# Top-k attention and two gated layers: transposes of later batches' keys written into the next block's search

## The chip, the core and the metric

The kernel runs on one core of a Trainium2 chip. The metric is the time of one execution in device microseconds (us). The core has TensorE (PE: matmuls and transposes), VectorE (DVE), ScalarE (ACT) and GpSimd (POOL); SyncE (SP) issues every DMA of this kernel, in one queue, in order. Matmuls write PSUM; the other engines copy from there to SBUF.

## What is computed

```python
scores = (q @ k^T) / sqrt(64)                  # 4 batches, 8 heads, 576 rows, head size 64
kth    = 32nd largest score of each row
attn   = softmax(where(scores >= kth, scores, -1e9))
x      = (attn @ v), laid out as 2304 rows x 512
y      = (sigmoid(x @ w_gate) * (x @ w_val)) @ w_out     # 512 -> 1536 -> 512
out    = relu(y @ w_in)**2 @ w_out2                      # 512 -> 2048 -> 512
```

## The kernel before

The 2304 rows are 18 tiles of 128 rows, grouped in 12 chunks (chunks 0 to 5 of one tile, 6 to 11 of two). In each chunk, attention goes over four pairs of heads. A **unit** is one row tile and one head: its scores (tile `sp`, L376) are copied to SBUF by ScalarE (`S`, L379), and VectorE searches them in a **block** of four maxima of eight (L392) with three replacements between (L399). Then come exponentials (ScalarE) and, from chunk 6 on, a split into float16 parts that ends as a DMA with transposition (`PT<-S`, L459), whose result is multiplied with the values (`xp`, L509). The two layers of chunk ci (`pg`, `pv`, `acc` in L753 and L793; `x2pq`, `ph`, `acc` in L825, L858 and L879) run on TensorE between the units of later chunks; their scaling needs squares on ScalarE (L823) that `x2pq` sums.

Before a batch's keys can be used, they are **prepared** once for each pair of heads by `prep_keys`: SP loads them (`kn` and the ends `ke`, L151 and L153), TensorE transposes them (`kpt`, L164: four transposes of 128 keys and one of 64), ScalarE rounds them to a high part (`kp`, L171), VectorE takes the low part (written over `kn`, L172), and SP stores both to DRAM (`ks`, L178). Units then load them as `kst` (L328). Batches 2 and 3 are prepared while chunks 6 and 8 are in attention, at the head of each pair of heads: eight preparations. They are called the first to the fourth (batch 2, TensorE at 438 to 524 us) and the fifth to the eighth (batch 3).

What sets the order: the program is traced as written, and a scheduler then places each instruction by priorities and by a timeline of its own; every engine and the DMA queue run what they were given in that order. A tile's name (its tag) has a fixed number of buffers: `S` has five, shared by the scores of units, by `kn` and by the values being prepared (`vm`); `kst` has three, shared by loaded keys and by `kp`; `qn` has two, shared by queries and `ke`. With five `S` buffers, `kn` of a preparation takes the buffer that the unit four blocks back gives up, when its transposing DMA has landed.

From chunk 6 on, the work traced with block n is put into its search by `late(marks)`, called once the four maxima exist (`marks`): first the float16 split of unit n-1, then `head(n + 1)` with the loads and scores of the next unit and with any preparation, then the values' preparation (`vn`, behind the fourth maximum), then the products of unit n-2. `add_manual_dep(..., NOSYNC)` orders two instructions for the scheduler; no engine waits for it on the chip.

Of the kernel before, what the change touches and what calls it, by code (L numbers as in the profile page):

```python
# [18 lines left out]
NOSYNC = mybir.DependencyInfo(mybir.DependencyClass.NoSync, mybir.DependencyReason.DATA)  # L19
# [39 lines left out]
MUP = 200.0  # L59
WSLOTS = 35  # L60
PREF = 4
YMOD = 0
LOP = 3
LOA = 0
# [9 lines left out]
def tile_topk_attention__then__two_moe_layers(  # L74
# [14 lines left out]
    nc = tc.nc  # L89
# [52 lines left out]
    kscr = {}  # L142
    kloc = {}

    def prep_keys(b, hp, keep=False):

        src = k[b, 2 * hp : 2 * hp + 2]
        kn = apool.tile([P, S], F32, tag="S", bufs=SB, name=f"kn_{b}_{hp}")
        kv = kn[:, 0 : CB * P].rearrange("p (c h d) -> p c h d", c=CB, h=2)
        for j in range(2):  # L150
            nc.sync.dma_start(kv[:, :, j], src[j, 0:SM].rearrange("(p c) d -> p c d", c=CB))  # L151
        ke = apool.tile([ST, 2, D], F32, tag="qn", bufs=2, name=f"ke_{b}_{hp}")
        nc.sync.dma_start(ke, src[:, SM:S].rearrange("h p d -> p h d"))  # L153
        kh = apool.tile([P, S], F32R, tag="kst", bufs=KST, name=f"kp_{b}_{hp}")
        kl = kn.bitcast(F32R)
        if keep:
            kl = mpool.tile([P, S], F32R, tag="m4", bufs=M4, name=f"kl_{b}_{hp}")
            kloc[(b, hp)] = (kh, kl)
        for lo, hi in ((0, CB), (CB, NB)):
            pt = ps_t.tile([P, 512], F32, tag="tr", name=f"kpt_{b}_{hp}_{lo}")  # L160
            w = 0
            for c in range(lo, hi):
                kp = P if c < CB else ST
                nc.tensor.transpose(  # L164
                    pt[:, w : w + kp],
                    (kv[:, c] if c < CB else ke).rearrange("p h d -> p (h d)"),
                    ident[0:kp, 0:kp],
                )
                w += kp
            c0 = lo * P  # L170
            nc.scalar.copy(kh[:, c0 : c0 + w], pt[:, 0:w])  # L171
            nc.vector.tensor_tensor(  # L172
                kl[:, c0 : c0 + w], pt[:, 0:w], kh[:, c0 : c0 + w], op=ALU.subtract
            )
        d = dpool.tile([2, 2, D, S], F32R, name=f"ks_{b}_{hp}", tag=f"ks_{b}_{hp}")
        for a, t in enumerate((kh.bitcast(F32), kl.bitcast(F32))):
            for j in range(2):
                nc.sync.dma_start(d.bitcast(F32)[j, a], t[j * D : (j + 1) * D])  # L178
        for j in range(2):
            kscr[(b, 2 * hp + j)] = d[j].rearrange("a d s -> (a d) s")  # L180
# [830 lines left out]
    def attention():  # L1011
# [21 lines left out]
        def head(n):  # L1033
# [3 lines left out]
            if j == 0 and i == 0:  # L1037
# [12 lines left out]
                for b in due:  # L1050
                    if (b, pr.hp) not in vscr:
                        prep_values(b, pr.hp)
                    if (b, pr.hp) not in done:
                        done.add((b, pr.hp))
                        prep_keys(b, pr.hp)
                if pr.ci == KEYS1 and (1, pr.hp) not in done:
                    done.add((1, pr.hp))
                    prep_keys(1, pr.hp)
# [58 lines left out]
        for n, (pr, pi, j, i) in enumerate(units):  # L1117
# [6 lines left out]
            if pr.ci >= TCI - 2:  # L1124

                def late(marks, n=n, pr=pr):
                    if units[n - 1][0].ci >= TCI:
                        turn(n - 1, marks[2])
                    if pr.ci >= TCI:
                        head(n + 1)  # L1130
                        if units[n - 1][0].ci < TCI:
                            tail(n - 1)
                    while late_values:
                        split_values(*late_values.pop(0), marks[3])
                    if units[n - 2][0].ci >= TCI:
                        tail(n - 2, marks[3])
# [153 lines left out]
```

## Time and profile before

| | |
|---|---|
| three runs | 1262.53, 1262.6 and 1261.23 us; median 1262.53 us |
| profiled execution | its span, first to last instruction, is 1261.3 us; the profile gives no other time for it |
| busy share of the span | PE 93%, DVE 76%, POOL 67%, ACT 66% |
| chain that ended last | PE 67%, ACT 9%, POOL 7%, DVE 7%, DMA 5% of the span |

The span is what the profiler saw on the core; the runs are timed without it. A busy share is an average over stages: VectorE's last search starts at 1070.92 us, and what follows its end is the last chunk's two layers on TensorE.

### The profile page before, as it was taken

The page shows a single profiled execution, that of the slowest core. Times are in us where ns is not written, and L with a number is a line of the kernel's source. Part 1 is how long each engine was busy: PE and PEld are TensorE (multiplying, and loading weights), DVE is VectorE, ACT ScalarE, POOL GpSimd, SP SyncE. Part 2 cuts the span into 40 slices and gives each one's busy share as a digit, 9 for nine tenths or more (in the row PEclk, how much of TensorE's full clock was granted, in tenths as well). Part 3 has the DMA queues.
Part 4 walks back from the last instruction along what each step waited for, and adds up shares of the span by engine and source line. Part 5 has one row for each costly group of instructions (what it writes and reads, how often), then busy time and mean ns, then how long its engine had stood idle before and what let it go on. Part 6 is the DMA issues. An engine that isn't in the chain of part 4 may idle for free.

```text
span 1261.3 us, 30690 instructions
## 1 busy us (share of the span) xinstructions
PE 1176.1 (93%) x11477; PEld 957.5 (76%) x11477; DVE 954.8 (76%) x1965; ACT 828.6 (66%) x1719; POOL 846.5 (67%) x1294
## 2 busy tenths in 40 slices
PE   6757989999889998899998999999999999999998
PEld 5536877987777877779787778877876887787775
DVE  6998789899977978899988899999789969110010
ACT  4998996577767676677776777776567657322122
POOL 1788774488876577797876987797678659425223
PEclk9986999999989999999999999999999999999999
DMA  7988762223344356665776575567434523200000
GB/s 188 366 298 275 260 199 81 59 76 90 113 131 130 81 125 159 143 136 130 137 157 133 125 181 115 127 140 158 77 73 97 116 54 60 53 2 1 17 1 18
DMA packets 243190, 153.94 MB, mean 122 GB/s; under 512 B 193120, under 2 KB 209504, under 8 KB 243040
## 3 DMA queue, kind: packets, MB, share of 16 engines
q1 hardware_dynamic: 243040, 151.97, 47.7%
q8 instruction: 91, 1.49, 0.5%
q14 instruction: 59, 0.48, 0.1%
HBM read 105.51 MB, written 18.09 MB: 98 GB/s over the span
## 4 chain that ended last, share of the span: by engine, by line
PE 67%; ACT 9%; POOL 7%; DVE 7%; DMA 5%; issue 3%; SPq 2%; POOLq 0%; ACTq 0%; DVEq 0%
PE ph L858 12%; PE acc L879 12%; PE acc L793 8%; PE pg L753 8%; PE pv L753 8%; PE sp L376 5%; PE xp L509 3%; DMA PT<-S 3%; DVE mx L392 2%; PE xp L536 2%; DVE W L399 2%; PE pg L912 1%; PE qpt L336 1%; PE ph L959 1%; PE acc L976 1%
## 5 line engine op out<-in xcount | busy, mean ns | idle before, releaser
L392 DVE MAX8 mx<-W 128x8 f32<-128x576 f32 x432 | 327.9, 759 | 11.2
L399 DVE MATCH_REPLACE8 W<-mx,W 128x576 f32<-128x576 f32 x288 | 213.8, 742 | 0.0
L858 PE MATMUL ph<-x,wi_w 128*128 128x256 f16 (+1 forms) x1920 | 190.9, 253 | 2.7 <-ACT x L832 2.6
L879 PE MATMUL acc<-w_w,rh 128*128 128x512 f16 x768 | 182.2, 379 | 0.9 <-POOL rh L871 0.9
L858 PEld LDWEIGHTS <-wi_w 128*128 128x128 f16 x1920 | 156.4, 99 | 29.0 <-issue 4.0
L753 PE MATMUL pg<-xs,wg_w 128*128 128x256 f16 (+1 forms) x1440 | 148.4, 254 | 1.1 <-ACT th L763 0.8
L753 PE MATMUL pv<-xs,wv_w 128*128 128x256 f16 (+1 forms) x1440 | 143.8, 252 | 5.1 <-DVE th L765 3.7
L376 PE MATMUL sp<-kst,qt 128*128 128x288 f32 x608 | 132.9, 330 | 6.5 <-ACT rh L869 2.5
L457 POOL TENSOR_TENSOR S<-W,S 128x512 f16<-128x512 f32 x192 | 137.0, 735 | 2.1
L379 ACT COPY S<-sp 128x576 f32<-128x576 f32 x144 | 91.8, 638 | 66.3 <-PE sp L376 39.7
L793 PEld LDWEIGHTS <-wo_w 128*128 128x128 f16 x1440 | 119.6, 99 | 19.2 <-issue 7.4
L411 ACT ACTIVATE W<-S,mx 128x576 f32<-128x576 f32 x144 | 111.8, 776 | 30.9 <-DVE mx L392 30.5
L753 PEld LDWEIGHTS <-wg_w 128*128 128x128 f16 x1440 | 118.9, 99 | 17.2 <-issue 1.4
L753 PEld LDWEIGHTS <-wv_w 128*128 128x128 f16 x1440 | 117.4, 98 | 18.1 <-issue 5.8
L765 DVE TENSOR_TENSOR th<-pv,th 128x512 f32<-128x512 f32 (+1 forms) x60 | 34.7, 579 | 125.4 <-PE pv L753 121.0
L879 PEld LDWEIGHTS <-rh 128*128 128x128 f16 x768 | 72.0, 98 | 73.3 <-POOL rh L871 1.2
L392 DVE MAX8 mx<-S 128x8 f32<-128x576 f32 x144 | 107.3, 745 | 25.9 <-ACT S L379 24.1
L793 PE MATMUL acc<-gh,wo_w 128*128 128x256 f16 (+1 forms) x1104 | 105.6, 250 | 4.7 <-ACT gh L768 2.6
L399 DVE MATCH_REPLACE8 W<-mx,S 128x576 f32<-128x576 f32 x144 | 106.9, 742 | 0.0
L455 POOL TENSOR_SCALAR W<-W,bs 128x576 f32<-128x576 f32 x96 | 71.6, 746 | 52.6 <-ACT S L454 47.8
L870 POOL TENSOR_TENSOR r<-r 128x512 f32<-128x512 f32 (+1 forms) x80 | 69.6, 869 | 54.8 <-ACT rh L869 54.1
L376 PEld LDWEIGHTS sp<-kst,qt 128*128 128x128 f32 x608 | 90.8, 192 | 17.5 <-issue 3.8
(246 smaller groups left out, 2331.5 us busy)
## 6 DMA issues: line engine op xcount, KB each, us to landing
kst<-ks SPq DMA_DIRECT2D x112, 288.0 KB, 3.1
v<-vd SPq DMA_DIRECT2D x32, 320.0 KB, 3.3
qn<-in_q_dram SPq DMA_DIRECT2D x128, 64.0 KB, 2.3
wi_r<-in_moe_w_in_dram SPq DMA_DIRECT2D x16, 512.0 KB, 6.2
w_r<-in_moe_w_out_dram SPq DMA_DIRECT2D x16, 512.0 KB, 4.5
v<-in_v_dram SPq DMA_DIRECT2D x56, 128.0 KB, 2.4
wg_r<-in_moe_w_gate_dram SPq DMA_DIRECT2D x12, 512.0 KB, 6.0
wv_r<-in_moe_w_val_dram SPq DMA_DIRECT2D x12, 512.0 KB, 7.3
```

What stands on the lines that cost most here:

```text
L376: nc.tensor.matmul(sp[:, e, 0:HALF], l, r, start=(x == 0), stop=(x == len(ops) - 1))
L379: nc.scalar.copy(ss.rearrange("p (e s) -> p e s", e=2), sp[:, :, 0:HALF])
L392: m8 = nc.vector.max(mx[:, min(r, 1)], cur)
L399: nc.vector.match_replace(wk, mx[:, min(r, 1)], cur, NEG)
L411: nc.scalar.activation(wk, ss, AF.Prelu, bias=kth, scale=-1.0, alpha=1.0 / BIG)
L455: nc.gpsimd.tensor_scalar(wk, wk, rz, 1.0, op0=ALU.mult, op1=ALU.mult)
L457: nc.gpsimd.tensor_tensor(pp[:, o : o + e - f], wk[:, f:e], pp[:, f:e], op=ALU.subtract)
L753: nc.tensor.matmul(pp[:, e * N : (e + 1) * N], wblk(wd, a, c, f0, P), xs[:, b_, c, :], start=(e == 0 and n == 0), stop=(n == 3 * KM - 1), ...
L793: nc.tensor.matmul(accs[d // 2][:, (d % 2) * N : (d % 2 + 1) * N], wblk("wo", a, f, d * P, P), gh[:, b_, e * N : (e + 1) * N], start=(f == ...
L858: nc.tensor.matmul(ph[:, e * N : (e + 1) * N], wblk("wi", a, c, f0, P), x2[:, b_, c, :], start=(e == 0 and n == 0), stop=(n == 3 * KM - 1) ...
L870: nc.gpsimd.tensor_tensor(r, r, r, op=ALU.mult)
L879: nc.tensor.matmul(acc2[i][:, 0:DM], gh[:, b_, e * N + i * P : e * N + (i + 1) * P], wblk("w2", a, f, 0, DM), start=(f == 0 and x == 0), s ...
```

## The change

`prep_keys` is cut in two for the preparations of batches 2 and 3 (`late=LATEK`): the loads stay where they were, and `split_keys` (transposes, rounding, low part, stores) is called in the same block's `late`, behind `head(n + 1)`, with the first transpose ordered behind the third maximum of block n (`marks[KMARK]`). So `kp` takes its buffer of tag `kst` after the keys that `head(n + 1)` loads, not before.

```diff
+LATEK = 1
+KMARK = 2
...
-    def prep_keys(b, hp, keep=False):
+    def prep_keys(b, hp, keep=False, late=False):
...
         nc.sync.dma_start(ke, src[:, SM:S].rearrange("h p d -> p h d"))
+        if late:
+            late_keys.append((b, hp, kn, kv, ke))
+        else:
+            split_keys(b, hp, kn, kv, ke, keep=keep)
+
+    late_keys = []
+
+    def split_keys(b, hp, kn, kv, ke, keep=False, after=None):
+
         kh = apool.tile([P, S], F32R, tag="kst", bufs=KST, name=f"kp_{b}_{hp}")
...
-                nc.tensor.transpose(
+                mm = nc.tensor.transpose(
...
+                if after is not None:
+                    tc.add_manual_dep(mm.ins, after.name, NOSYNC, reason="landed by then")
+                    after = None
...
-                        prep_keys(b, pr.hp)
+                        prep_keys(b, pr.hp, late=LATEK)
...
+                    while late_keys:
+                        split_keys(*late_keys.pop(0), after=marks[KMARK])
                     while late_values:
```

Nothing is removed or added in count on the compute engines. The order is the same up to the first preparation. In names, the first number of `kn`, `ke`, `kpt`, `kp`, `ks`, `vm`, `ve` is the batch and the second the pair of heads; in `S`, `sp`, `PT` it is row tile and head; `kst` begins with the chunk; the last number only counts.

The DMA queue at the first preparation (loads of `kn_2_0`, batch 2, pair 0); before:

```order
L151 DMA kn_2_0_5957<-in_k_dram 128x4x64 x2
L153 DMA ke_2_0_5960<-in_k_dram 64x2x64
L196 DMA ve_2_0_5948<-in_v_dram 64x2x64 x2
L310 DMA v_6_0_1_5710<-vd_1_0_3603 128x1280
L300 DMA qn_6_1_5979<-in_q_dram 128x2x64 x2
L300 DMA qn_7_1_5982<-in_q_dram 128x2x64 x2
L178 DMA ks_2_0_5974<-kp_2_0_5962 64x576 x2
L178 DMA ks_2_0_5974<-kn_2_0_5957 64x576 x2
L328 DMA kst_6_1_1_5987<-ks_1_0_773 128x576
L328 DMA kst_6_2_1_6121<-ks_1_1_973 128x576
```

and after the change:

```order
L342 DMA kst_6_1_1_5970<-ks_1_0_773 128x576
L330 DMA v_5_3_1_5348<-in_v_dram 128x256
L333 DMA v_5_3_1_5348<-in_v_dram 64x64
L330 DMA v_5_3_1_5348<-in_v_dram 128x256
L333 DMA v_5_3_1_5348<-in_v_dram 64x64
L207 DMA vm_2_0_5945<-in_v_dram 128x256 x2
L153 DMA kn_2_0_5957<-in_k_dram 128x4x64 x2
L155 DMA ke_2_0_5960<-in_k_dram 64x2x64
L210 DMA ve_2_0_5948<-in_v_dram 64x2x64 x2
L324 DMA v_6_0_1_5710<-vd_1_0_3603 128x1280
L314 DMA qn_6_1_5962<-in_q_dram 128x2x64 x2
L342 DMA kst_6_2_1_6121<-ks_1_1_973 128x576
```

The load of the second head's keys (`kst_6_1`) stood behind the stores of the first preparation and now stands ahead of its loads.

TensorE at the same preparation, from the last of the sums `x2pq` on; before:

```order
L825 LDWEIGHTS ones_86
L825 MATMUL x2pq_3_5654<-x2_3_5653,ones_86 128x128
L477 MATMUL tp_5_6_5997<-ident_81,W_5_6_5846 128x128 x4
L214 LDWEIGHTS ones_86
L214 MATMUL vn_2_0_6012<-vs_2_0_5953,ones_86 128x1
L214 LDWEIGHTS ones_86
L214 MATMUL vn_2_0_6012<-vs_2_0_5953,ones_86 128x1
```

and the scores of head 1 of the same row tile, 50 rows further down:

```order
L858 LDWEIGHTS wi_w0_2973
L858 MATMUL ph_3_1_5745<-x2_3_5653,wi_w0_2973 128x128
L858 LDWEIGHTS wi_w0_2973
L858 MATMUL ph_3_1_5745<-x2_3_5653,wi_w0_2973 128x128
L376 MATMUL sp_6_1_6124<-kst_6_1_1_5987,qt_6_0_1_5819 128x288 x4
L536 MATMUL xp_5_3_6141<-PE_5_3_6137,v_5_3_1_5348 64x128 x2
```

after the change, from the same sum on:

```order
L839 LDWEIGHTS ones_86
L839 MATMUL x2pq_3_5654<-x2_3_5653,ones_86 128x128
L390 MATMUL sp_7_1_6339<-kst_6_1_1_5970,qt_7_0_1_5941 128x288 x4
L228 LDWEIGHTS ones_86
L228 MATMUL vn_2_0_6012<-vs_2_0_5953,ones_86 128x1
L228 LDWEIGHTS ones_86
L228 MATMUL vn_2_0_6012<-vs_2_0_5953,ones_86 128x1
L491 MATMUL tp_5_7_6131<-ident_81,W_5_7_5986 128x128 x4
```

Scores of a later unit (`sp_7_1`) now stand between the sums and `vn`, those of `sp_7_0` between the last transposes of the preparation, and `sp_6_1` stands some 190 rows earlier than it did.

The DMA queue at the second preparation (`kn_2_1`); before:

```order
L196 DMA ve_2_2_6861<-in_v_dram 64x2x64
L459 DMA_TRANSPOSE PT_6_0_6229<-S_6_0_5989 128x9x128
L196 DMA ve_2_2_6861<-in_v_dram 64x2x64
L151 DMA kn_2_1_6392<-in_k_dram 128x4x64 x2
L459 DMA_TRANSPOSE PT_6_1_6336<-S_6_1_6123 128x9x128
L328 DMA kst_6_3_1_6422<-ks_1_1_973 128x576
L300 DMA qn_7_2_6417<-in_q_dram 128x2x64 x2
L459 DMA_TRANSPOSE PT_7_0_6371<-S_7_0_6231 128x9x128
L178 DMA ks_2_1_6409<-kp_2_1_6397 64x576 x2
L178 DMA ks_2_1_6409<-kn_2_1_6392 64x576 x2
```

after:

```order
L155 DMA ke_2_1_6395<-in_k_dram 64x2x64
L314 DMA qn_6_2_6397<-in_q_dram 128x2x64 x2
L210 DMA ve_2_2_6861<-in_v_dram 64x2x64 x2
L473 DMA_TRANSPOSE PT_6_0_6229<-S_6_0_5972 128x9x128
L473 DMA_TRANSPOSE PT_6_1_6336<-S_6_1_6123 128x9x128
L153 DMA kn_2_1_6392<-in_k_dram 128x4x64 x2
L473 DMA_TRANSPOSE PT_7_0_6371<-S_7_0_6231 128x9x128
L314 DMA qn_7_2_6400<-in_q_dram 128x2x64 x2
L192 DMA ks_2_1_6426<-kp_2_1_6414 64x576 x2
```

The transposing DMA of row tile 6, head 1 (`PT_6_1`) stood behind the keys' load and now stands ahead of it.

At the third preparation, the queue has `ke_2_2`, `PT_6_2`, a load of values, a load of queries, `kn_2_2` before, and `PT_6_2`, `ke_2_2`, a load of value ends, `kn_2_2` after. At the fourth, one load of queries and one of value ends stand between `kn_2_3` and `PT_6_5` before, and two of each after. The first transposes of the second, third and fourth preparations stand in rows 4039, 4682 and 5387 of TensorE before, and in rows 4010, 4521 and 5286 after; ahead of them stand 34, 82 and 48 fewer matmuls of the two layers (counted in widths of 128 columns), and 26 to 122 fewer at the four of batch 3. On ScalarE at the sixth preparation (`kn_3_1`), the copy of the next block's scores stood ahead of the second half of the squares for `x2pq`, with the roundings `kp` and the previous unit's float16 part around it; now float16 part, copy and roundings all stand ahead of the first half, and the copy of the block after that between the halves.

## Rows read from the trace of the kernel before

**Rows 1.** The page: span, then each engine's busy time, share and instructions.
```profile
span 1261.3 us, 30690 instructions
...
PE 1176.1 (93%) x11477; PEld 957.5 (76%) x11477; DVE 954.8 (76%) x1965; ACT 828.6 (66%) x1719; POOL 846.5 (67%) x1294
```

**Rows 2.** Stretches of 25 us: busy PE, PEld, DVE, ACT, POOL; granted clock, DMA share, GB/s.
```profile
475.00:500.00 25.00, 21.32 (x309) 18.62 (x308) 21.07 (x49) 17.98 (x44) 19.47 (x36) 0.96 0.61 147
...
675.00:700.00 25.00, 21.84 (x218) 18.31 (x218) 21.66 (x50) 18.26 (x40) 17.93 (x29) 1.00 0.67 133
...
750.00:775.00 25.00, 25.00 (x261) 22.09 (x259) 24.42 (x51) 17.56 (x37) 19.70 (x36) 1.00 0.70 160
```

**Rows 3.** TensorE waits from 400 to 800 us: total, times, longest.
```profile
PE kpt L164 <- DMA kn<-in_k_dram: 5.5, 3, 2.8
```

**Rows 4.** Timeline of TensorE: start, us, instructions; in brackets the idle time before.
```profile
443.05 0.65 PE L477 MATMUL tp<-ident,W 128*128 128x128 f32 x4 [1.16 <-POOL W L441]
...
469.41 0.63 PE L164 MATMUL kpt<-ident,kn 128*128 128x128 f32 x4 [0.57 <-DMA kn<-in_k_dram]
...
496.91 0.63 PE L164 MATMUL kpt<-ident,kn 128*128 128x128 f32 x4 [2.80 <-DMA kn<-in_k_dram]
...
523.70 0.66 PE L164 MATMUL kpt<-ident,kn 128*128 128x128 f32 x4 [2.16 <-DMA kn<-in_k_dram]
...
529.84 0.77 PE L376 MATMUL sp<-kst,qt 128*128 128x288 f32 x4 [2.50 <-ACT rh L869]
...
660.65 0.76 PE L376 MATMUL sp<-kst,qt 128*128 128x288 f32 x4 [0.97 <-DMA kst<-ks]
...
683.78 0.38 PE L825 MATMUL x2pq<-x,ones 128*128 128x256 bf16 x2 [1.47 <-ACT x L823]
...
685.54 2.24 PE L753 MATMUL pv<-xs,wv_w 128*128 128x256 f16 x19 [0.47 <-ACT th L763]
```

**Rows 5.** Stretches of 2 us behind the longest wait.
```profile
498.00:500.00 2.00, 2.00 (x25) 2.00 (x23) 1.16 (x3) 1.59 (x5) 0.67 (x1) 0.55 0.88 224
500.00:502.00 2.00, 2.00 (x25) 2.00 (x24) 1.24 (x3) 0.30 (x1) 0.00 (x0) 0.59 0.81 226
```

**Rows 6.** Timeline of VectorE: first maximum of four blocks.
```profile
438.59 0.74 DVE L392 MAX8 mx<-S 128x8 f32<-128x576 f32 x1
...
449.10 0.76 DVE L392 MAX8 mx<-S 128x8 f32<-128x576 f32 x1 [2.86 <-ACT S L379]
...
471.22 0.76 DVE L392 MAX8 mx<-S 128x8 f32<-128x576 f32 x1 [4.17 <-ACT S L379]
...
499.66 0.76 DVE L392 MAX8 mx<-S 128x8 f32<-128x576 f32 x1 [0.64 <-ACT S L379]
```

**Rows 7.** Timeline of the DMA queue: issues, start and us to issue.
```profile
444.01 1.07 SPq L328 DMA_DIRECT2D kst<-ks  x2
...
465.45 1.48 SPq L151 DMA_DIRECT2D kn<-in_k_dram  x2
...
467.05 1.29 SPq L459 DMA_TRANSPOSE PT<-S  x1
...
487.90 0.69 SPq L153 DMA_DIRECT2D ke<-in_k_dram  x1
```

**Rows 8.** Chain that ended last, 455 to 475 us: a transfer and its landing.
```profile
462.07 3.37 DMA PT<-S
```

**Rows 9.** Timeline of GpSimd: the operand of the second transposing transfer.
```profile
464.76 1.43 POOL L457 TENSOR_TENSOR S<-W,S 128x512 f16<-128x512 f32 x2
```

**Rows 10.** Timeline of ScalarE: copies of the scores out of PSUM.
```profile
448.43 0.64 ACT L379 COPY S<-sp 128x576 f32<-128x576 f32 x1 [0.90 <-PE sp L376]
...
681.93 0.64 ACT L379 COPY S<-sp 128x576 f32<-128x576 f32 x1 [3.30 <-DMA PT<-S]
```

**Rows 11.** Timeline of TensorE: two groups of 24 matmuls, back to back.
```profile
491.16 1.50 PE L753 MATMUL pg<-xs,wg_w 128*128 128x128 f16 x24
492.50 1.50 PE L753 MATMUL pv<-xs,wv_w 128*128 128x128 f16 x24
```

## The prediction

> **What bounds the kernel now.** The page comes first: TensorE is busy for 1176.1 of 1261.3 us, and no other engine is above 76% [rows 1]. So the time is TensorE's work plus its gaps, and the question is where the gaps are. The stretches of 25 us answer it: around the first four preparations TensorE is busy for 21 of 25 us, at the sixth for 22, and from 750 us on for all 25 [rows 2]. What the change wins or loses has to happen between 430 and 725 us; behind that, TensorE has no gap left to close until its last chunks, so a gain or loss goes through to the end unaltered.
>
> The list of waits in that part is headed by the very instruction that is moved: transposes of keys, 5.5 us in 3 waits [rows 3]. The timeline shows them at the second, third and fourth preparation: 0.57, 2.80 and 2.16 us [rows 4]. Behind the 2.80 us the granted clock is 0.55 and 0.59 for 4 us, where 2.4 GHz would be 1.00 and 1.2 GHz 0.50 [rows 5]: work done there took 2 x 0.45 + 2 x 0.41 = 1.7 us longer.
>
> VectorE shows the other side. The blocks behind a preparation start late: it waits 2.86 us for scores at the first, 4.17 at the second [rows 6]. At the first, the scores come late because TensorE does them late [rows 10]: their keys are issued at 444.01, behind the stores [rows 7]. At the second, two transposing transfers set the pace: the first is issued at 462.07 and lands 3.37 us later [rows 8], at 465.44; the keys, which take its buffer, are issued at 465.45, and only then, at 467.05, the second transfer, although its operand was ready at 464.76 + 1.43 = 466.19 [rows 7, 9].
>
> **The change, part by part.** Work: the same transposes, copies, subtractions and stores, so nothing in busy time. All of the effect is order.
>
> Loads of keys past the preparation: at the first preparation `kst_6_1` no longer waits for the stores, and its scores stand far ahead. The 2.86 us of VectorE's wait should go, so all of attention behind it comes 2.86 earlier. TensorE also gets a group of scores into the gap where it waited 1.16 us [rows 4]; that is worth up to 1.2 us there, but see below why I don't add it.
>
> The transposes: the change is said to put them later, so that the keys have landed. The order says otherwise. Ahead of the transposes of the second, third and fourth preparation stand 34, 82 and 48 fewer matmuls of the layers. 24 of these take 492.50 - 491.16 = 1.34 us, 0.056 each [rows 11]: TensorE reaches the transposes 1.9, 4.6 and 2.7 us sooner by its own work. The third maximum is an order for the scheduler alone. What counts on the chip is when the keys land, and their loads are bound to the landing of a transposing transfer [rows 7, 8].
>
> How much earlier do keys land? Second preparation: 2.86 from attention, less 1.29 for the transfer that now goes ahead of them [rows 7], is 1.6. Third: 2.86, plus 0.86 because that transfer goes at 466.19 and not at 467.05, plus 0.69 since `ke` no longer stands ahead of the next one [rows 7], is 4.4. Fourth: 4.4 again.
>
> Now step by step. Second: TensorE arrives at least 1.9 earlier, the keys 1.6; a wait remains, so the transposes run 1.6 earlier. Third: between the two lies 4.6 - 1.9 = 2.7 us less work, so arrival is 4.3 earlier and the keys 4.4; the wait stays at 2.7, and the clock falls behind it as before. Fourth: 1.9 more work, so arrival is 4.4 - 1.9 = 2.5 earlier, the keys 4.4; the wait shrinks to 2.16 - 1.9 = 0.3. The transposes run 4.4 earlier, of which 2.7 is work that is still to come: a net of **-1.7 us**. As long as a wait is left at the fourth, whatever TensorE gains before it only lengthens that wait, which is why the gap at the first preparation isn't added. The bounds: if attention gains nothing, 4.6 us of order shift at the third turn into waiting (+4.6); if the keys always come in time, the three waits, the slow clock and the gap go, 5.5 + 1.7 + 1.2 = -8.4.
>
> The DMA page of the Trainium skill ("DMA: Bandwidth & Descriptors", Rules for kernel authors) says to issue a transfer early and wait for it late, so that its fixed cost is overlapped. Rows and order agree with its first half only: issue stays, and the waiting instruction comes no later. By the rule this part would be worth the whole -8.4; by the order it is -1.7.
>
> Past the fourth preparation: one more load of queries and one of value ends stand ahead of the transposing transfer that the next scores wait for; at 0.69 for such an issue [rows 7] this is 1.4 later, and the scores' wait of 2.50 [rows 4] could grow by that. The row names ScalarE's work as what ended it, not the transfer, so I take half, **+0.7** (between -2.5, if ScalarE's new order frees it sooner, and +1.4).
>
> Batch 3: the wait of 0.97 for keys at 660.65 [rows 4] goes, as loads stand ahead of stores now: **-1.0** (0 if the same transfer is late for another reason). At the sixth preparation ScalarE is held 3.30 us by a copy whose buffer isn't free [rows 10], and TensorE waits 1.47 and 0.47 us for ScalarE's squares and its gate [rows 4]. The copy now stands ahead of both halves of the squares, but further ahead; the next block's copy stands between the halves and can hold them again. I take half of 1.9, **-1.0** (0 to -1.9). Order moves there by 1.5 to 6.8 us (26 to 122 matmuls), but before the change TensorE doesn't wait for keys there, and ScalarE's new order lets each unit's float16 part go ahead of the held copy, so I count no new wait.
>
> What is moved past what: stores go later behind the transfers of two units; nobody reads them before the next chunk, 16 units on. The transposes' buffer `kn` is held longer; the next values take it a pair later. `ke` shares two buffers with queries, so the second load of queries waits for the last transpose in the DMA queue, as it did.
>
> Sum: -1.7 + 0.7 - 1.0 - 1.0 = -3.0 us. The profiled execution's span of 1261.3 would become 1258.3; it lies 1.2 under the median of the runs, and against the median of 1262.53 I forecast **1259.5 us**.
>
> **Rivals.** *Attention doesn't follow* (slower). Order has moved attention's work ahead in TensorE's queue by up to 4.6 us; if blocks don't come earlier, TensorE stands at the third preparation for 2.8 + 4.6. For it: transfers, which order can't hurry, set the pace [rows 7, 8]. Against it: the 2.86 us hung on one load that is moved. Price: 4.6, and 1.4 from the queue behind the fourth, is 1262.5 + 6.0 = 1268.5. It decides if VectorE's wait behind the first preparation stays above some 1.5 us.
>
> *The buffers are the bound* (the same time). Behind the second preparation VectorE waits for a transposing transfer to give back a buffer of `S` [rows 6, 7], and there are five as before. Each wait then changes its place: net 0, 1262.5. The Trainium skill says of regular gaps that there may not be enough memory for the next tile ("Perfetto Trace Analysis", Optimization Strategy); the gaps here agree in being regular, one for each preparation. Against it: the queue's order adds to the gap (0.86 us of it at the second), and that order changes.
>
> *The keys come in time* (a larger gain). If attention wins more than I count, say the whole 4.17 of the second block too [rows 6], keys are 2.86 + 4.17 = 7.0 earlier at the third and ahead of TensorE's arrival. Then -8.4 - 1.0 - 1.0, with the wait at 529.84 as it is: 1262.5 - 10.4 = 1252.1.
>
> **How the numbers follow.** My forecast has a chance of 0.46, with a range of its own of 1256 to 1262 (its terms moved half way to their bounds); the larger gain 0.12, the same time 0.21, slower 0.21. The three runs lie within 0.1%; 0.2%, 2.5 us, is about what can be told from no change. Of my forecast's own range some four fifths, 0.37, lie below 1260.0 and the rest, 0.09, within 0.2%. Faster is then 0.37 + 0.12 = 0.49, the same 0.09 + 0.21 = 0.30, slower 0.21. The range for 8 in 10 runs from 1251.5 to 1267.5: it takes in the larger gain's 1252.1 and most of the slower case, which lies around 1268.5 and below, where attention follows in part.
>
> **What would show it.** Right: VectorE waits under 1 us for the second block behind the first preparation; transposes of keys still wait, about 2 us at the second, 2.7 at the third, little at the fourth; no wait for keys at the fifth preparation; TensorE's gaps between 430 and 725 us are 2 to 3 us shorter. Wrong: no wait at the third preparation (then more is won), or one of 5 us and more there, or gaps in TensorE's stretches behind 725 us, where I expect none.

## The result and the profile after

The changed kernel's median is 1270.06 us over 4 runs (1265.89 to 1271.98) against 1262.57 for the kernel before: ratio 1.0066, 95% interval 1.0044 to 1.0088. It is slower, by 0.7%. 1259.5 was forecast; the range ended at 1267.5. Lines of the changed kernel carry new numbers: `kpt` is L175, `sp` L390, the copy of scores L393, `acc` of layer 2 L893, `kn` is loaded in L153.

The profiled execution is the fastest of the four, 2.8 us longer than the one of [rows 1]. Page, span and busy time:

```profile
span 1264.1 us, 30675 instructions
...
PE 1171.0 (93%) x11477; PEld 952.4 (75%) x11477; DVE 959.1 (76%) x1965; ACT 828.4 (66%) x1719; POOL 846.3 (67%) x1294
```

Stretches of 25 us, columns as in [rows 2]:

```profile
475.00:500.00 25.00, 22.59 (x338) 19.05 (x335) 20.39 (x46) 18.07 (x46) 20.21 (x38) 1.00 0.71 169
675.00:700.00 25.00, 21.99 (x223) 18.22 (x222) 21.77 (x51) 18.21 (x40) 15.01 (x26) 1.00 0.62 139
725.00:750.00 25.00, 22.60 (x149) 13.27 (x148) 18.41 (x42) 15.35 (x34) 20.87 (x33) 0.93 0.59 133
750.00:775.00 25.00, 25.00 (x256) 21.65 (x254) 24.07 (x50) 18.90 (x40) 19.36 (x36) 1.00 0.74 145
```

The third line is the new one: a gap and a slow clock behind 725 us, where the prediction expected no gap. Before the change it was:

```profile
725.00:750.00 25.00, 25.00 (x212) 17.01 (x210) 23.46 (x52) 19.42 (x44) 20.77 (x34) 1.00 0.68 152
```

What TensorE waits for, as in [rows 3] (total, times, longest):

```profile
PE kpt L175 <- DMA kn<-in_k_dram: 7.1, 4, 2.4
PE sp L390 <- ACT S L393: 4.5, 7, 1.2
PE acc L893 <- POOL rh L885: 3.1, 3, 2.4
```

TensorE's timeline, the rows that answer to [rows 4]:

```profile
461.73 1.57 PE L893 MATMUL acc<-w_w,rh 128*128 128x512 f16 x6 [2.42 <-POOL rh L885]
...
494.37 0.63 PE L175 MATMUL kpt<-ident,kn 128*128 128x128 f32 x4 [1.30 <-DMA kn<-in_k_dram]
...
521.37 0.66 PE L175 MATMUL kpt<-ident,kn 128*128 128x128 f32 x4 [2.23 <-DMA kn<-in_k_dram]
...
654.62 0.80 PE L390 MATMUL sp<-kst,qt 128*128 128x288 f32 x4 [1.10 <-ACT S L393]
...
673.38 0.63 PE L175 MATMUL kpt<-ident,kn 128*128 128x128 f32 x4 [1.16 <-DMA kn<-in_k_dram]
...
676.58 0.80 PE L390 MATMUL sp<-kst,qt 128*128 128x288 f32 x4 [0.63 <-ACT S L393]
...
681.57 0.38 PE L839 MATMUL x2pq<-x,ones 128*128 128x256 bf16 x2 [0.78 <-ACT x L837]
...
683.58 0.80 PE L390 MATMUL sp<-kst,qt 128*128 128x288 f32 x4 [1.24 <-ACT S L393]
...
732.98 1.08 PE L175 MATMUL kpt<-ident,kn 128*128 128x128 f32 x4 [2.40 <-DMA kn<-in_k_dram]
```

Waits for keys have moved from the second, third and fourth preparation to the third, fourth, sixth and eighth. At the end of the last one the clock falls (TensorE's busy time, then the other engines'; the clock is the third number from the right):

```profile
730.00:732.00 2.00, 0.57 (x6) 0.27 (x3) 0.99 (x2) 0.96 (x2) 1.89 (x4) 1.00 0.56 127
732.00:734.00 2.00, 1.02 (x5) 0.72 (x5) 0.16 (x1) 0.78 (x1) 1.92 (x4) 0.66 0.91 181
734.00:736.00 2.00, 2.00 (x7) 0.91 (x7) 0.82 (x2) 1.90 (x6) 1.92 (x4) 0.50 0.28 63
736.00:738.00 2.00, 2.00 (x10) 0.88 (x9) 1.32 (x3) 0.61 (x2) 1.81 (x3) 0.99 0.24 53
```

2 x 0.34 + 2 x 0.50 = 1.7 us are lost to the clock (some 0.2 of it while TensorE still stands) and 2.4 to the wait: some 4 us at one place. Why the keys were late is in the DMA queue. First the kernel before at the eighth preparation, then the changed kernel; the last row of the first is TensorE's, that of the changed kernel stands above, at 732.98:

```profile
728.63 1.29 SPq L459 DMA_TRANSPOSE PT<-S  x1
...
731.89 1.29 SPq L151 DMA_DIRECT2D kn<-in_k_dram  x2
...
737.63 0.60 PE L164 MATMUL kpt<-ident,kn 128*128 128x128 f32 x4
```

```profile
724.28 0.38 SPq L324 DMA_DIRECT2D v<-vd  x1
724.76 1.34 SPq L473 DMA_TRANSPOSE PT<-S  x1
729.02 1.29 SPq L153 DMA_DIRECT2D kn<-in_k_dram  x2
```

In the changed kernel the transposes start as soon as the keys are there, 732.98 - 729.02 = 3.96 us behind their issue. At that rate keys were there at 735.85 before the change (the trace of before has the second load landing at 735.8), and TensorE came at 737.63: 1.8 us of **slack**, the time for which an operand lies ready before it is used. With the change TensorE is free for them at 732.98 - 2.40 = 730.58, 7.05 sooner; 6.8 of it are the 122 matmuls that now stand behind. The keys are issued only 2.87 sooner. So the wait of 2.4 is made up of 7.05 - 2.87 - 1.8.

### The profile page after: what moved, and what is told of

The parts are those of the page before. It is cut to its first block, busy times and chain, and to the rows that moved or that the text cites. A ratio compares the mean times of both kernels' runs of the same rounds, so it can differ in the third digit from the quotient of the medians.

```text
span 1264.1 us, 30675 instructions
## 1 busy us (share of the span) xinstructions
PE 1171.0 (93%) x11477; PEld 952.4 (75%) x11477; DVE 959.1 (76%) x1965; ACT 828.4 (66%) x1719; POOL 846.3 (67%) x1294
## 4 chain that ended last, share of the span: by engine, by line
PE 61%; DVE 12%; ACT 9%; POOL 7%; DMA 5%; issue 3%; SPq 2%; ACTq 0%; POOLq 0%; DVEq 0%
PE ph L872 11%; PE acc L893 11%; PE acc L807 7%; PE pv L767 7%; PE pg L767 7%; PE sp L390 4%; DVE mx L406 4%; DVE W L413 4%; PE xp L523 3%; DMA PT<-S 2%; PE xp L550 1%; PE pg L926 1%; POOL S L471 1%; PE ph L973 1%; PE acc L990 1%
## 5 line engine op out<-in xcount | busy, mean ns | idle before, releaser
L893 PE MATMUL acc<-w_w,rh 128*128 128x512 f16 x768 | 182.5, 381 | 3.1 <-POOL rh L885 3.1
L767 PE MATMUL pg<-xs,wg_w 128*128 128x256 f16 (+1 forms) x1440 | 144.7, 252 | 0.7 <-ACT th L777 0.7
L390 PE MATMUL sp<-kst,qt 128*128 128x288 f32 x608 | 133.4, 330 | 7.0 <-ACT S L393 4.8
L767 PEld LDWEIGHTS <-wv_w 128*128 128x128 f16 x1440 | 117.5, 99 | 18.9 <-issue 6.3
L393 ACT COPY S<-sp 128x576 f32<-128x576 f32 x144 | 92.0, 639 | 59.4 <-PE sp L390 31.6
L893 PEld LDWEIGHTS <-rh 128*128 128x128 f16 x768 | 72.7, 98 | 76.1 <-POOL rh L885 3.9
L390 PEld LDWEIGHTS sp<-kst,qt 128*128 128x128 f32 x608 | 90.6, 192 | 18.0 <-ACT S L393 7.1
```

Source lines behind the costliest of these rows:

```text
L390: nc.tensor.matmul(sp[:, e, 0:HALF], l, r, start=(x == 0), stop=(x == len(ops) - 1))
L393: nc.scalar.copy(ss.rearrange("p (e s) -> p e s", e=2), sp[:, :, 0:HALF])
L767: nc.tensor.matmul(pp[:, e * N : (e + 1) * N], wblk(wd, a, c, f0, P), xs[:, b_, c, :], start=(e == 0 and n == 0), stop=(n == 3 * KM - 1), ...
L893: nc.tensor.matmul(acc2[i][:, 0:DM], gh[:, b_, e * N + i * P : e * N + (i + 1) * P], wblk("w2", a, f, 0, DM), start=(f == 0 and x == 0), s ...
```

## The experiments

Two measures are used. The first is the ratio to the kernel before, whose runs were made on the same chip; groups with different medians of before ran apart from each other, so their times are compared by the ratio. The second is worked out from the one trace kept of each kernel: the idle time ahead of every instruction of TensorE, and (1 - granted clock) x time, each summed over batch 2 (430 to 640 us) and batch 3 (640 to 800 us). "Order" is by how many of the layers' matmuls the keys' transposes stand later (+) or sooner (-) in TensorE's order than before the change, first to eighth preparation.

```
kernel         order, batch 2    batch 3           median  before  ratio [95% interval]
changed        0 -34 -82 -48     -26 -64 -82 -122  1270.06 1262.57 1.0066 [1.0044, 1.0088]
again          the same                            1270.15 1263.88 1.0051 [1.0037, 1.0064]
batch2         0 -34 -82 -48     -80 -32 -4 +18    1264.12 1263.88 1.0010 [1.0000, 1.0020]
batch3         0 0 0 0           +44 +12 -6 +14    1263.47 1263.88 1.0002 [0.9991, 1.0013]
next_block     +50 +72 +83 +72   +102 +58 +92 +70  1272.74 1263.88 1.0072 [1.0058, 1.0085]
eighth_later   0 -34 -82 -48     -26 -64 -82 +28   1265.58 1264.65 1.0009 [0.9995, 1.0022]
eighth_prompt  0 -34 -82 -48     -26 -64 -82 -122  1269.04 1264.65 1.0035 [1.0022, 1.0048]
batch3_fourth  0 -34 -82 -48     +6 -36 -46 -72    1265.44 1264.65 1.0005 [0.9990, 1.0020]
batch3_next    0 -34 -82 -48     +46 +14 -30 -10   1266.65 1264.65 1.0021 [1.0009, 1.0033]
loads_only     -20 0 -54 -24     -80 -100 -148 -138 1269.67 1264.03 1.0043 [1.0028, 1.0059]
loads_only_2   the same                            1268.95 1263.58 1.0045 [1.0028, 1.0061]
late34         0 0 0 0           0 0 0 0           1262.60 1264.03 0.9989 [0.9979, 1.0000]
late1          0 -33 -12 0       0 0 0 0           1266.02 1264.03 1.0016 [1.0006, 1.0026]
not_first      0 0 -33 -24       +20 -12 -14 +22   1267.79 1264.03 1.0022 [1.0011, 1.0033]
fill8          0 -34 -82 -48     -26 -64 -82 -144  1268.62 1263.58 1.0039 [1.0026, 1.0053]
late_but_same  0 0 0 0           +44 +12 -6 +14    1262.85 1263.58 0.9996 [0.9984, 1.0009]
```

```
trace          batch 2: idle + clock     batch 3: idle + clock
before         15.8 + 3.4 = 19.2         4.3 + 0   = 4.3
changed        16.3 + 1.7 = 18.0         7.7 + 1.7 = 9.4
again          17.7 + 1.7 = 19.4         7.7 + 3.4 = 11.1
batch2         14.3 + 5.1 = 19.4         4.7 + 0   = 4.7
batch3         15.3 + 1.7 = 17.0         6.8 + 0   = 6.8
next_block     22.0 + 5.1 = 27.1         2.4 + 1.7 = 4.1
eighth_later   16.3 + 5.1 = 21.4         5.4 + 1.7 = 7.1
eighth_prompt  17.2 + 5.1 = 22.3         6.8 + 1.7 = 8.5
batch3_fourth  16.5 + 1.7 = 18.2         5.6 + 1.7 = 7.3
batch3_next    16.0 + 3.4 = 19.4         4.4 + 1.7 = 6.1
loads_only     14.9 + 3.4 = 18.3         4.0 + 0   = 4.0
loads_only_2   18.9 + 3.4 = 22.3         4.8 + 0   = 4.8
late34         13.8 + 5.1 = 18.9         4.3 + 0   = 4.3
late1          19.5 + 5.1 = 24.6         4.5 + 0   = 4.5
not_first      18.7 + 6.8 = 25.5         3.4 + 0   = 3.4
fill8          16.4 + 5.1 = 21.5         6.1 + 1.7 = 7.8 (filler not counted)
late_but_same  13.4 + 5.1 = 18.5         6.0 + 0   = 6.0
```

The theory is "order ahead of supply": TensorE reaches keys and scores sooner than they are fed. The rivals are "only the eighth preparation", "buffers" (keys hold a buffer of `S` for longer), and "late tracing itself".

**again**: the changed kernel once more.

> The changed kernel, unchanged, once more. Its profile of 1265.9 us shows only 2.8 us more than before, its other runs 4 to 7 more, so a second profile is wanted. Order ahead of supply (the theory): TensorE reaches scores and transposes 2 to 7 us sooner than they are fed, stands, and the clock falls to 1.2 GHz behind the longer waits, more often in the slower executions: 1266 to 1272 us, with slow clock at two or three places between 440 and 740 us, and waits for ScalarE's copies of scores and for keys of 10 us and more. Only the 8th preparation (rival): the loss stands behind 725 us alone, 3 us in each profile, and what is more is spread evenly.

Measured: 1270.15 us. The wait at the eighth preparation is there again, 2.27 us at 735.19 (the view names ScalarE as what ended it, but the keys landed at 735.05), with a slow clock behind it, and another slow stretch at 685 us, behind a wait of 1.22 us for a copy of scores. Keys and scores hold TensorE 5.0 + 2.3 + 3.6 us between 400 and 1000 us. Batch 3 costs 5.1 us (changed) and 6.8 us (again) more than before; batch 2 costs the same, 18.0 and 19.4 against 19.2. The execution profiled in again is its median, and its span is 7.1 us longer than before: batch 3 is nearly all of it.

**batch2 and batch3**: the late transposes for one batch.

```diff
-                        prep_keys(b, pr.hp, late=LATEK)
+                        prep_keys(b, pr.hp, late=LATEK and b == 2)
```

In batch3 it is `b == 3`.

> Transposes are late for batch 2 alone; for batch 3 they stand with the loads as before. In TensorE's order the keys of batch 2 stand 0, 34, 82 and 48 matmuls sooner than before (as with the full change), those of batch 3 80, 32, 4 sooner and 18 later. Order ahead of supply: the loss of batch 2 stays and that at the 8th preparation goes, 1264 to 1267 us. Only the 8th preparation: nothing is left of the loss, 1262 to 1263.

> Transposes are late for batch 3 alone; all of batch 2 is as before, and the keys of batch 3 stand 44 and 12 matmuls later, 6 sooner, 14 later than before. Order ahead of supply: what makes the loss is the order, and here it isn't ahead, so no new wait: 1260 to 1263 us. Only the 8th preparation (late transposes and a load of values ahead of the transposing transfer): the loss is there, 1265 to 1270. If the buffers of keys are the cause (stores later, kn held longer), 1265 too.

Measured: next to nothing in either, so the two halves don't add up to the 0.5 to 0.7% of the whole. The order says why: with one half alone, batch 3's keys stand where they stood at the seventh preparation, to 6 matmuls, and later at the eighth. That fits both the theory and the first rival; only late tracing as a cost of its own is spoken against (batch3 has it in four preparations).

**next_block**: all late transposes one block later.

```diff
-                    while late_keys:
-                        split_keys(*late_keys.pop(0), after=marks[KMARK])
+                    while late_keys and late_keys[0][0] < n:
+                        split_keys(*late_keys.pop(0)[1:], after=marks[2])
...
```

The first entry of an item of `late_keys` is here, in eighth_later and in batch3_next the unit with which it was loaded; in batch3_fourth it is the batch.

> The late transposes are made one block later still, behind the third maximum of the block after. In TensorE's order keys stand 50 to 102 matmuls later than before the change, 3 to 6 us. Order ahead of supply: keys have landed by then, the 5.5 us of waits for keys go with the slow clock behind them: 1255 to 1261 us. Buffers (rival): kn keeps its buffer of S a block longer, so copies of scores wait for one and TensorE for the copies: 1268 us and more, with ScalarE's copies held by the landing of a transposing transfer.

Measured: slower, 1.0072. The theory's number failed, though half of its account holds: TensorE no longer waits for keys between 400 and 800 us. The rival's waits stand in their place, from 430 to 800 us:

```profile
ACT S L394 <- DMA PT<-S: 34.4, 19, 4.2
...
PE xp L524 <- DMA PT<-S: 8.3, 4, 3.3
PE sp L391 <- ACT S L394: 7.3, 5, 4.4
```

ScalarE's copies wait 34.4 us for a buffer of `S` that a transposing transfer still reads. Before the change it was 23.3:

```profile
ACT S L379 <- DMA PT<-S: 23.3, 13, 3.4
```

So a late place in the order has a price as well: a buffer of keys that is held a block longer costs batch 2 some 8 us (27.1 against 19.2).

**eighth_later and eighth_prompt**: the eighth preparation alone is moved, or alone isn't late.

```diff
-                    while late_keys:
-                        split_keys(*late_keys.pop(0), after=marks[KMARK])
+                    while late_keys and (not (late_keys[0][1:3] == (3, 3)) or late_keys[0][0] < n):
+                        u, kb, khp, *ks = late_keys.pop(0)
+                        split_keys(kb, khp, *ks, after=marks[2 if u < n else KMARK])
...
```
```diff
-                        prep_keys(b, pr.hp, late=LATEK)
+                        prep_keys(b, pr.hp, late=LATEK and (b, pr.hp) != (3, 3))
```

> The change, but the transposes of the 8th preparation alone are traced one block later, behind the third maximum of the next block. In TensorE's order they stand 28 matmuls later than before the change and not 122 sooner; the seven others stand as in the changed kernel. In the changed kernel TensorE waits 2.3 to 2.4 us there with some 2 us of slow clock behind it, in sum 4.3 us between the same points of its work. Order ahead of supply: both go, 1265 to 1267 us, no wait for keys behind 725 us, granted clock 1.00 from 725 to 750. Buffers (rival; kn held one block longer, as in next_block): a wait for ScalarE's copy or for a transposing transfer of 3 us and more takes its place, 1269 to 1273 us.

> The change, but the 8th preparation's transposes are traced with their loads, as before the change. Their place in TensorE's order stays 122 matmuls ahead of before, and SyncE's order up to the keys' loads (value load ahead of the transposing transfer) stays too; only the stores go ahead of later loads. Order ahead of supply: place and supply are those of the changed kernel, so the wait of 2.4 us and the slow clock stay, 1268 to 1272 us. If the late tracing of this step is itself the cause (rival): 1264 to 1267 us.

Measured: 1.0009 and 1.0035. The other seven preparations stand in the order as in the changed kernel in both. TensorE's timeline and the stretch behind 725 us in eighth_later:

```profile
746.49 0.60 PE L176 MATMUL kpt<-ident,kn 128*128 128x128 f32 x4
```

```profile
725.00:750.00 25.00, 24.50 (x207) 16.67 (x206) 19.87 (x44) 17.09 (x40) 23.02 (x39) 1.00 0.53 119
```

There is no wait, and the clock stays at 1.00. In eighth_prompt, with the same place in the order and prompt tracing, the wait is there (1.87 us at 737.72, clock 0.93 from 725 to 750), and its interval overlaps that of again. In eighth_later one wait of 0.50 us for a copy of scores stands in its stead. The two ran on one chip, so their medians can be set against each other: 1269.04 - 1265.58 = 3.5 us, close to the some 4 that the rows give for this place (against again, on another chip, the ratios give 5.3). So most of the loss hangs on the eighth preparation's place in the order, not on its late tracing.

**batch3_fourth and batch3_next**: batch 3 behind the fourth maximum, or one block later.

```diff
-                        split_keys(*late_keys.pop(0), after=marks[KMARK])
+                        m = marks[3 if late_keys[0][0] == 3 else KMARK]
+                        split_keys(*late_keys.pop(0), after=m)
```
```diff
+                    while late_keys and (not (late_keys[0][1] == 3) or late_keys[0][0] < n):
+                        u, kb, khp, *ks = late_keys.pop(0)
+                        split_keys(kb, khp, *ks, after=marks[2 if u < n else KMARK])
...
```

> The change, but batch 3's transposes are ordered behind the fourth maximum and not the third. Batch 2 stays; the keys of batch 3 stand 6 matmuls later and 36, 46 and 72 sooner than before (with the change 26, 64, 82 and 122 sooner). Order ahead of supply: 50 matmuls at the 8th are 2.8 us, more than its wait of 2.4, so wait and slow clock go there, and the 6th's wait of 1.2 to 1.5 falls by the 28 matmuls' 1.6: 1263 to 1266 us. Buffers: kn is held longer by a quarter of a block, 1270 or more.

> The change, but all of batch 3's transposes stand one block later (keys 46 and 14 matmuls later than before, 30 and 10 sooner). Order ahead of supply: no wait for keys in batch 3, 1262 to 1265 us. Buffers: each of the four holds its buffer of S a block longer; in next_block batch 3 lost some 2 us between the same points, so 1264 to 1266 us with waits for transposing transfers, and no slow clock at the 8th.

Measured: 1.0005 and 1.0021. 1266.65 for batch3_next lies above both ranges, and its one profile, of its fastest run (1263.99), can't show where the 2 us are. The wait for keys at the eighth is gone in both. In the profile of batch3_fourth a wait for scores took its place, with the slow clock:

```profile
742.43 0.40 PE L390 MATMUL sp<-kst,qt 128*128 128x288 f32 x1 [2.27 <-ACT S L393]
```

So in this execution TensorE reaches attention's next operand too soon as well, and not the keys alone. The runs of this kernel lie from 1259.5 to 1269.4, so this wait need not be in each of them.

**loads_only** (and loads_only_2): in the kernel before, the second head's keys are loaded ahead of the preparation; nothing is late.

```diff
...
+                if due:
+                    pr.load_keys(1)
                 for b in due:
...
-            if i == 0 and j == 0:
+            if i == 0 and j == 0 and not due:
                 pr.load_keys(1)
```

> The kernel before with one edit: in a block that prepares keys, the load of the pair's second head of keys is traced ahead of the preparation; transposes and all else stay with their loads, none is late. The keys then stand 20, 0, 54, 24 (batch 2) and 80, 100, 148, 138 matmuls (batch 3) sooner in TensorE's order than before. Order ahead of supply: late tracing isn't needed for the loss, and batch 3's order is further ahead than the changed kernel's, 8.3 us at the 7th: waits for keys at the 7th and 8th preparation with slow clock, 1268 to 1275 us. Late tracing is the cause (rival): 1261 to 1264 us.

> The kernel of loads_only once more, for a profile of another execution; its runs lay from 1262.5 to 1274.7 us and its profile was that of 1262.5, with the clock at 1.00 behind 525 us and waits for keys of 0.6 to 1.1 us in batch 3. If slow clock behind such waits makes the difference: a run of 1267 us or more shows waits of the same number, some of them longer, and two to four stretches of slow clock more, 1.7 us each. If something else does: the same clock and the difference in one gap.

Measured: 1.0043 and 1.0045. One moved load puts attention ahead in the order and makes a loss of the full change's size, so late tracing isn't needed for one. That it is the same loss isn't shown, for its place was forecast wrong. Batch 3's order is further ahead than in the changed kernel, and yet TensorE waits there for keys only 0.4 to 1.5 us at a time, with the clock at 1.00: in the first profile keys are issued at 726.67, 5.2 us sooner than before and not 2.9. Here supply nearly kept up. Of the second profile's 6.9 us over before, 3.1 are in batch 2 (22.3) and 0.5 in batch 3; the rest isn't placed by this measure. Slow clock doesn't make the difference between the two executions, 1260.7 and 1268.2 us of span: it is 3.4 us in both. Idle time in batch 2 is 14.9 against 18.9. TensorE runs the same instructions in the same order in both, so the places can be named: the wait for keys at the second preparation is 0.57 and 2.24 us, and at 578 us a wait of 1.81 for a transposing transfer is in the second alone. What starts the difference is open.

**late34, late1, not_first, late_but_same**: the late transposes for some preparations, by the same edit as batch2, with `b == 2 and pr.hp >= 2`, `b == 2 and pr.hp == 0`, `b == 3 or pr.hp >= 1` and `b == 3 or pr.hp >= 2` in the place of `b == 2`.

> Late transposes at the third and fourth preparation alone. Loads of keys go ahead of stores there, but TensorE's order has all eight preparations' keys where they stood before, to the matmul. Order ahead of supply: without a shift no new wait and the old ones stay: within 2 us of before. Late tracing itself (rival, kn held longer): 1266 and more. Loads ahead of stores are worth time by themselves: 1259 to 1261 us.

> Late transposes at the first preparation alone, the one behind which VectorE waited 2.86 us. Keys stand 0, 33 and 12 matmuls sooner at the first three and as before from the fourth on, batch 3 as before. Order ahead of supply: VectorE's wait goes, TensorE's wait for GpSimd's halves of layer 2 (2.4 us at 461 us with the change, 0.6 before) and its slow clock come in its place, and both are made up by the fourth, whose order is as before: within 2 us of before. If attention's start alone counts: 1258 to 1260 us.

> The change at all preparations but the first. Keys stand 0, 0, 33, 24 sooner in batch 2; 20 later, 12 and 14 sooner and 22 later in batch 3. Seven of eight preparations are late, but the order isn't ahead by more than 1.9 us anywhere. Order ahead of supply: no wait for keys behind 725 us, 1261 to 1265 us. Late tracing itself (rival): nearly the whole loss, 1268 to 1270.

> Late transposes at the third and fourth preparation of batch 2 (late34) and all four of batch 3 (batch3). Keys stand as before in batch 2 and 44 and 12 later, 6 sooner, 14 later in batch 3. Order ahead of supply: no loss, the gain of late34 (0.1%) and the nothing of batch3 together, 1260 to 1264 us where before has 1264. Late tracing itself (rival): 1267 and more.

Measured: 0.9989, 1.0016, 1.0022, 0.9996. Where TensorE's order isn't ahead (late34 and late_but_same, and batch3 above), late tracing and early loads cost nothing, in two, six and four preparations; late34 is 1.4 us faster than before, at the edge of its interval, and the fastest of all. late1 and not_first, with 33 matmuls ahead in batch 2, lose 0.2%. But the size of a loss doesn't follow the number of matmuls: batch2, eighth_later and batch3_fourth have 82 at the third preparation and lose 0.1% or less. not_first was expected at 1261 to 1265 and came at 1267.8, next to the rival's 1268 to 1270; what speaks against that rival is late_but_same, with one late preparation less and no loss. As expected no transposes of keys wait behind 725 us, and batch 3 costs 3.4; the loss is in batch 2 (25.5, 6.8 of it slow clock).

**fill8**: TensorE is kept busy through the wait.

```diff
             w = 0
+            if (b, hp) == (3, 3) and lo == 0:
+                for x in range(24):
+                    mm = nc.tensor.transpose(pt[:, 0:P], ident, ident)
...
```

> The changed kernel with 24 added transposes of the identity right ahead of the 8th preparation's, into the same buffer, which the real ones then overwrite: work whose result isn't used, some 24 x 0.14 = 3.4 us of it by the spacing of the real ones. The 8th preparation then stands 144 matmuls sooner than before, not 122. If wait and slow clock both count: TensorE would have stood 2.4 + 1.2 us, the filler takes 3.4 of it, so the wait is gone and the clock stays at 1.00; the kernel gains the 1.7 us of slow clock and no more, 1268 us against 1270. If the clock falls for another reason: 0.5 to 0.7 behind the filler too and 1270 or more. If the wait alone made the loss: 1270.

Measured: 1268.62 us, 1.0039. The timeline, and the clock behind the wait:

```profile
734.50 2.78 PE L175 MATMUL kpt<-ident 128*128 128x128 f32 x24
737.69 0.63 PE L180 MATMUL kpt<-ident,kn 128*128 128x128 f32 x4 [0.41 <-DMA kn<-in_k_dram]
```

```profile
736.00:738.00 2.00, 1.59 (x15) 1.39 (x14) 0.17 (x1) 1.45 (x2) 1.81 (x3) 1.00 0.78 165
738.00:740.00 2.00, 2.00 (x18) 1.50 (x17) 0.00 (x0) 1.80 (x5) 2.00 (x4) 1.00 0.65 131
```

TensorE does useless work instead of standing, and the slow clock behind the eighth is gone (a wait of 1.32 us for scores follows at 747.11, with the clock at 1.00). That the clock falls because TensorE stands agrees with the rows: it fell at this wait in the traces of changed, again and eighth_prompt, and it stayed at 1.00 in the one execution where the filler took the wait's place. The time doesn't show the gain: 1.5 us less than again would agree with the 1.7 that were expected, but the intervals overlap, and eighth_prompt, with wait and slow clock, is at 1.0035.

## Why the prediction was wrong

**The step that failed** is in the terms for batch 3: "Order moves there by 1.5 to 6.8 us (26 to 122 matmuls), but before the change TensorE doesn't wait for keys there, [...] so I count no new wait." No wait is not the same as slack enough. By the landings in the trace of before, keys lay ready 0.3, 0.3, 0.1 and 1.8 us ahead of TensorE at the fifth to the eighth preparation. At the eighth the order moves by 6.8, so the step should have asked that keys come 5 us sooner there. They came 2.9 sooner, and the price was some 4 us, paid as wait and as slow clock. At the sixth TensorE was there 5.1 us sooner (3.6 of it by the order's 64 matmuls), the keys 3.8: a wait of 1.16. And ScalarE's copies of scores, for which no new wait was counted either, hold TensorE 1.10, 0.63 and 1.24 us at 654.62, 676.58 and 683.58. Batch 3 was forecast at -2.0 and measured at +5.1 and +6.8. eighth_later takes the one place out: it is 0.9 us above before, where eighth_prompt, on the same chip and with the wait, is 4.4 above. With the wait the loss was 6.3 in again and 7.5 in the first runs, so up to some 3 us of it are not this place's; in again's trace the sixth's wait, now 1.52, and the slow clock at 685 us stand beside it.

**Batch 2** was forecast at -1.7 and +0.7, -1.0 in sum. The profiles of changed and again give -1.2 and +0.2. In all eight traces with this order in batch 2 (changed, again, batch2, eighth_later, eighth_prompt, batch3_fourth, batch3_next, fill8) it costs 18.0 to 22.3, 20.0 in the mean, against 17.0 to 19.2, 18.4 in the mean, in the four with the old order (before, batch3, late34, late_but_same): no gain is seen, and if anything a loss. That changed came near the sum is luck, for its terms didn't come true. Of the working, VectorE's wait of 2.86 us did go (its block starts at 444.58 without one). The keys didn't follow it: forecast 1.6, 4.4 and 4.4 us sooner at the second, third and fourth preparation, they were issued 1.6 later, 1.8 and 2.3 sooner. Before (the second is in [rows 7]):

```profile
491.94 1.28 SPq L151 DMA_DIRECT2D kn<-in_k_dram  x2
...
519.98 1.28 SPq L151 DMA_DIRECT2D kn<-in_k_dram  x2
```

and in the changed kernel:

```profile
467.08 1.27 SPq L153 DMA_DIRECT2D kn<-in_k_dram  x2
...
490.10 1.77 SPq L153 DMA_DIRECT2D kn<-in_k_dram  x2
...
517.64 1.28 SPq L153 DMA_DIRECT2D kn<-in_k_dram  x2
```

The single waits were missed: forecast some 2, 2.7 and 0.3 us at the second, third and fourth, measured 0, 1.30 and 2.23. The scores' wait of 2.50 behind the fourth, which was to grow by 0.7, fell to 0.40. And a wait that was in no term came up, 2.42 us for GpSimd's half of `rh` at 461.73 (0.59 before): GpSimd had two scalings of attention's rows (0.75 us each) and a split of x (1.17 us) in front of it.

**The wait for `kst` at the fifth** (-1.0) went as said, and gave nothing: TensorE waits 1.10 us for ScalarE's copy of the scores in its stead. **The squares at the sixth** (-1.0): the wait for `x2pq` fell from 1.47 to 0.78, in the direction forecast, but 1.16 for keys stands beside it now.

**The rivals.** "Attention doesn't follow" gave 1268.5 and is the nearest. Its mechanism is the one that the runs showed, its place is not: it was put at the third preparation and tied to VectorE's wait behind the first, which went. Attention followed as far as the seventh preparation (its keys are issued 6.1 us sooner, 697.66 against 703.79) and fell back at the eighth. The rows say where it fell back. The keys take the buffer of a transposing transfer, whose operand ScalarE and GpSimd make. ScalarE begins its part 6.0 us sooner than before (719.17 against 725.14). GpSimd is then still at the split of prepared values (719.27 to 720.81), begins its first step 5.1 sooner and its second 4.0, because a step of layer 2 (`r`) now stands between the two. Before:

```profile
726.18 0.75 POOL L455 TENSOR_SCALAR W<-W,bs 128x576 f32<-128x576 f32 x1
...
727.16 1.44 POOL L457 TENSOR_TENSOR S<-W,S 128x512 f16<-128x512 f32 x2
```

and in the changed kernel:

```profile
721.06 0.74 POOL L469 TENSOR_SCALAR W<-W,bs 128x576 f32<-128x576 f32 x1
721.77 1.03 POOL L884 TENSOR_TENSOR r<-r 128x512 f32<-128x512 f32 x1
...
723.15 1.43 POOL L471 TENSOR_TENSOR S<-W,S 128x512 f16<-128x512 f32 x2
```

The transfer itself, issued 3.9 sooner (724.76 against 728.63), took 4.19 us to land, and 3.20 before. The chain that ended last shows it and the keys behind it:

```profile
724.76 4.19 DMA PT<-S
...
729.69 3.15 DMA kn<-in_k_dram
...
732.98 1.38 PE kpt L175 x5
```

So 2.9 of the 6.0 us were left for the keys. Why the transfer took longer is open; in again it took 4.32. The load of values ahead of it cost next to nothing: its operand was ready at 723.15 + 1.43 = 724.58. "The buffers are the bound" is true of next_block, where keys hold theirs a block longer.

**Two readings in the prediction** don't hold, though nothing hangs on them: TensorE is busy for 21 of 25 us in one stretch around the first four preparations, 475 to 500, and for 22.4 to 23.6 in the others from 425 to 550; and its terms, all moved half way to their bounds, give 1254 to 1264 and not 1256 to 1262.

The Trainium skill's rule to issue a transfer early and wait for it late ("DMA: Bandwidth & Descriptors", Rules for kernel authors) was worth nothing that can be measured by itself. next_block follows it in all eight preparations, has no wait for keys left, and is at 1.0072; late_but_same, where TensorE comes 12 to 44 matmuls later at three preparations, is at 0.9996.

## What to carry to other kernels

When an edit moves work in the order of the engine that bounds the kernel, put three numbers beside each other at every place that moves: how much sooner the engine gets there (by the order, and by what it has gained up to there), how much slack its operand had before (landing against use, also where nothing waited), and how much sooner the operand itself comes. A wait appears where the first exceeds the sum of the others: 7.05 against 1.8 + 2.9 at the eighth, 5.1 against 0.3 + 3.8 at the sixth. The order alone would have missed the sixth (3.6). A wait costs its own length and, behind some of 2 us, the slow clock too. Holding the operand's buffer longer to avoid it has a price of its own: at one place it was worth it (eighth_later), at all eight it cost more than it saved (next_block).

## What the runs showed of the hardware

The clock's losses came in one size: in all seventeen traces they add up to multiples of 1.7 us over batch 2 and over batch 3 (the granted clock is then 0.50, 1.2 GHz). Which wait brings one can't be told from its length: behind 2.40 us at 732.98 and 2.42 us at 461.73 the clock fell, behind 2.23 us at 521.37 and, before the change, 2.50 us at 529.84 [rows 4] it stayed at 1.00, and before the change it fell at 444 us, where the longest wait is 1.16 us among several short ones. One program's runs can lie further apart than the three of before that were shown first, 0.1%: 35 later ones of the same kernel on one chip lie from 1259.8 to 1269.0 us, loads_only's twelve from 1262.5 to 1274.7. Between its two profiled executions idle time differs and the clock doesn't, and why is open.
